# Two of twelve attention chunks rounded later, feature differences moved from GpSimd to VectorE, a feature store and the sums' roundings at other places in the order

## The chip, the cores and the metric

The kernel runs on one core of a Trainium2 chip. The time is device microseconds (us) of one execution, and the time of a kernel is the median of several executions. Engines go by the names of the profile: PE is TensorE, ACT is ScalarE, DVE is VectorE, POOL is GpSimd, SP is the engine that issues nearly all DMAs here. Each engine takes its instructions in the order of the program; an instruction that waits holds up those behind it on its engine.

## The reference

A retention layer (linear attention with a decay per head), then two feed-forward layers on its output. All arithmetic is float32.

```python
for t in range(S):                       # B=2, H=8, S=768, D=64
    state = gamma[None, :, None, None] * state + einsum('bhd,bhe->bhde', k[:, :, t], v[:, :, t])
    y[:, :, t] = scale * einsum('bhd,bhde->bhe', q[:, :, t], state)
x = y.transpose(0, 2, 1, 3).reshape(B * S, H * D)      # 1536 tokens x 512
h = x @ w_in;  x = (h / (1 + exp(-h))) @ w_out         # 512 -> 2048 -> 512
h = x @ moe2_w_in;  return maximum(0.01 * h, h) @ moe2_w_out
```

## The kernel before, in words

The program's order is written out by hand: within an engine, instructions run in the order in which the source issues them, and tiles bring the waits.

**Number format.** A float32 operand is cut into a high part and a rest that PE multiplies separately (`halves`, L199: an ACT copy writes the high part, a DVE subtraction the rest), and three of the four products are taken. The weights arrive as 64-bit words and are turned into float32 on the chip: `words` (L140, two ACT copies, into a buffer of the list `rt` and into the one tile `u`), `clamp` (L148, two DVE operations), `sign` (L159, DVE), `low` (L166, DVE; it reads `u`). `rt` holds three buffers `r`; `rt.pop(0)` takes the one that has been free longest in list order. What is not needed at once goes to a scratch tensor in DRAM (`keep_w`, `keep_s`) and is fetched again (`fetch_w`).

**Stage 1, attention** (to about 52 us): twelve chunks of 128 tokens, two at a time: scores on PE, masking on DVE (L273), values, states and outer products on PE. `store_x` (L355) takes the result of a chunk: for the first six it is scaled by DVE into SBUF (L363), for the last six it stays in PSUM; then it is rounded by `halves`. Chunks 4 and 5 (counting from 0) are the last two of the second set of three, whose halves go to places `w` and `xb`.

**Stage 2, first products of layer 0** (about 52 to 172 us): eight steps, each 256 of the 2048 features for all 1536 tokens. Steps 0 and 1 are computed plainly (`plain`, L863): for each half `p` of the tokens four groups of 12 matmuls, into the two double banks `p0` and `p1` and four single banks `b0` to `b3`. A group's result is read by ACT (L439, the activation); the next step writes the same banks. Steps 2 to 7 (`rest`, L890) use seven products in place of eight: they need sums and differences of weight blocks (`sums`, L192, four operations on POOL) and of the input (`first_t`, `rest_t`, L341 and L346: two operations each, rounded by `split_t`, L351, into `tt`). `up_tasks` (L797) lists what each step does beside its matmuls, by position 0 to 7: a task is issued ahead of the matmuls of its position, and so ahead of the ACT reading of that position's result. Step 1 ends with the first product of step 2 (`n.go(1)`), into the double bank `p0`.

**Stage 3, second products of layer 0** (172 to 304 us) reads the features of a step back from DRAM (`keep` stores them, 1.5 MB; `fetch_g` reads 0.5 MB).

**Stage 4, first products of layer 1** (304 to 426 us): step 0 plain, the others with seven products. In each step `words(w)` of a later weight is at position 2.

**Stage 5, second products of layer 1** (`Two.run`, L561; 426 us to the end): units of about 5.5 us in the first eight, which are plain; the later units use sums of weights that `keep_s` stored, which `ask(k)` fetches into `sf` or `u` and two operations (ACT L648, DVE L654) round.

Of the kernel before, what the change touches and what calls it, by code (L numbers as in the profile page):

```python
# [9 lines left out]
F32 = mybir.dt.float32  # L10
# [8 lines left out]
C = 128  # L19
# [15 lines left out]
PLACES = 6  # L35
NCST = NP * C + C + H + H + NP
# [6 lines left out]
def retention_moe_kernel(ctx: ExitStack, tc: tile.TileContext, att, w1, w2, cst, out):  # L43
# [44 lines left out]
    gate = sb.tile([128, 1], F32, name="gate")  # L88
# [51 lines left out]
    def words(w, which=(0, 1)):  # L140
        t = stage[w]
        if 0 in which:
            r = rs[w] = rt.pop(0)
            nc.scalar.activation(out=r.bitcast(F32), in_=t[:, :, :, 1].bitcast(F32), func=AF.Abs)  # L144
# [47 lines left out]
    def sums(w, which=range(4)):  # L192
        A21, A22, A11, A12 = (blocks(w)[:, n] for n in range(4))
        S1, S2, S3, S4 = (sf[:, n] for n in range(4))
        for o, a, b, op in [((S1, A21, A22, ALU.add), (S3, A11, A21, ALU.subtract),
                             (S2, S1, A11, ALU.subtract), (S4, A12, S2, ALU.subtract))[n] for n in which]:
            nc.gpsimd.tensor_tensor(out=o, in0=a, in1=b, op=op)  # L197
# [157 lines left out]
    def store_x(j):  # L355
# [6 lines left out]
        if j < LATE:  # L362
            nc.vector.tensor_tensor(out=f, in0=y, in1=g4(G), op=ALU.mult)  # L363
            y = f
        if s % 2 == 0:
# [4 lines left out]
        if j >= LATE:  # L370
            nc.scalar.activation(out=f, in_=y, func=AF.Copy)
# [121 lines left out]
    class Two:  # L493
# [67 lines left out]
        def run(self):  # L561
# [67 lines left out]

            for n in range(self.UNITS):  # L630
# [15 lines left out]
                if 1 <= n <= Q:  # L646
                    k = n - 1
# [5 lines left out]
                if 1 <= n <= Q:  # L653
                    nc.vector.tensor_tensor(out=S[k][1], in0=hold[k % 2], in1=S[k][0].bitcast(F32), op=ALU.subtract)  # L654
                for k in range(2) if n == 0 else [n + 1] if n + 1 < Q else []:
                    ask(k)
# [13 lines left out]
    with tc.manual_schedule():  # L670
# [71 lines left out]
        def left_a():  # L742

# [3 lines left out]
            nc.gpsimd.tensor_copy(out=gate, in_=l[:, 1, 511:512].bitcast(F32))  # L747
# [4 lines left out]
            4: lambda: (load_next(), clamp(wb)), 5: lambda: signed(wb),  # L752
# [44 lines left out]
        def up_tasks(layer, k):  # L797
            t = [[] for _ in range(8)]
            at = lambda n, *f: t[n].extend(f)
            if layer == 0 and k < 2:  # L800
                wd = first_w[3]
                if k == 0:
                    at(0, lambda: low(wb), lambda: first_t(0, nc.gpsimd), lambda: rest_t(0, nc.gpsimd))
                    at(1, lambda: words(wc), lambda: split_a(wb))
                    at(2, lambda: clamp(wc), lambda: signed(wc))
                    at(3, lambda: low(wc), lambda: sums(wc))
                    at(4, lambda: split_t(0, 0), lambda: first_t(1, nc.vector))
                    at(6, lambda: split_t(1, 0))
                else:
                    at(0, lambda: split_t(0, 1), lambda: rest_t(1, nc.vector))  # L810
                    at(2, lambda: split_a(wc), lambda: words(wd))
                    at(3, lambda: split_s(wc))
                    at(4, lambda: split_t(1, 1), lambda: clamp(wd))
                    at(5, lambda: signed(wd))
                    at(6, lambda: low(wd), lambda: sums(wd))
                return t
            if layer == 0:
# [5 lines left out]
                if k + 2 < Q:  # L823
# [4 lines left out]
                    at(4, lambda: (low(b), sums(b)), lambda: words(w, (0,)))  # L828
# [14 lines left out]
            if k == 0:  # L843
                at(0, lambda: fetch_w(n), lambda: first_t(1, nc.vector), lambda: rest_t(1, nc.gpsimd))
# [4 lines left out]
                at(7, lambda: split_t(1, 1), lambda: sums(m))  # L849
                return t  # L850
# [242 lines left out]
```

## Time and profile before

| | us |
|---|---|
| median of 3 executions | 559.93 |
| lowest, highest | 558.67, 561.56 |
| the profiled execution, its own time | 561.33 |
| span of the profiled execution, first to last instruction | 559.5 |
| TensorE busy in it | 542.5 |

The own time of the profiled execution lies 1.8 us above its span and 1.4 us above the median. TensorE's granted clock was 0.992 of full speed on average over the span. Busy shares say little of what a change is worth where an engine is nearly always busy; the idle time in front of its instructions, and who ended it, says more.

### The profile page before, as it was taken

The page shows a single profiled execution, that of the slowest core. Times are in us where ns is not written, and L with a number is a line of the kernel's source. Part 1 is how long each engine was busy: PE and PEld are TensorE (multiplying, and loading weights), DVE is VectorE, ACT ScalarE, POOL GpSimd, SP SyncE. Part 2 cuts the span into 40 slices and gives each one's busy share as a digit, 9 for nine tenths or more (in the row PEclk, how much of TensorE's full clock was granted, in tenths as well). Part 3 has the DMA queues.
Part 4 walks back from the last instruction along what each step waited for, and adds up shares of the span by engine and source line. Part 5 has one row for each costly group of instructions (what it writes and reads, how often), then busy time and mean ns, then how long its engine had stood idle before and what let it go on. Part 6 is the DMA issues. An engine that isn't in the chain of part 4 may idle for free.

```text
span 559.5 us, 8890 instructions
## 1 busy us (share of the span) xinstructions
PE 542.5 (97%) x3546; PEld 503.0 (90%) x3546; DVE 417.6 (75%) x546; ACT 301.8 (54%) x367; POOL 104.7 (19%) x92
## 2 busy tenths in 40 slices
PE   7989999999999999999999999998999979999996
PEld 6878999999998788888888999998999858999996
DVE  3798787999956687664867677767877278898993
ACT  2135586777774566644445376646765166443440
POOL 2585322333300000000600662202200000000000
PEclk8999999999999999999999999999999989999999
DMA  8982335778767977889274427776747986642521
GB/s 319 406 336 78 137 127 193 281 266 283 256 227 266 406 237 241 251 289 293 83 255 164 183 114 301 294 293 223 281 150 258 382 311 220 197 136 77 183 82 39
DMA packets 41789, 127.54 MB, mean 228 GB/s; under 512 B 3730, under 2 KB 12050, under 8 KB 39700
## 3 DMA queue, kind: packets, MB, share of 16 engines
q1 hardware_dynamic: 41456, 126.63, 63.8%
q8 instruction: 28, 0.46, 0.3%
q10 hardware_dynamic: 292, 0.34, 0.2%
q14 instruction: 13, 0.11, 0.1%
HBM read 85.01 MB, written 41.94 MB: 227 GB/s over the span
## 4 chain that ended last, share of the span: by engine, by line
PE 58%; DVE 17%; DMA 11%; ACT 5%; issue 5%; POOL 2%; SPq 1%; DVEq 0%; ACTq 0%; POOLq 0%
PE p L394 12%; PE b L394 9%; PE b L602 8%; PE p L471 6%; PE b L471 6%; PE p L602 6%; DMA scr<-r 4%; PE b L878 3%; DVE w L201 3%; DMA c<-g 2%; PE p L878 2%; PE p L586 2%; DVE r L168 2%; PE b L586 2%; DMA sf<-scrs 2%
## 5 line engine op out<-in xcount | busy, mean ns | idle before, releaser
L394 PE MATMUL p<-tt,w 128*128 128x384 f32 x468 | 87.9, 335 | 2.2 <-ACT c L426 2.2
L394 PEld LDWEIGHTS p<-tt,w 128*128 128x128 f32 x468 | 81.8, 188 | 2.9 <-ACT c L426 2.8
L471 PE MATMUL b<-w,wt 128*128 128x512 f32 x216 | 55.1, 390 | 0.5 <-DVE wt L201 0.5
L471 PE MATMUL p<-w,wt 128*128 128x512 f32 x216 | 54.8, 389 | 0.0
L201 DVE TENSOR_TENSOR w<-c,w 128x1024 fp32r<-128x1024 f32 x23 | 29.7, 1293 | 28.9 <-ACT w L200 28.9
L146 ACT ACTIVATE u<-ws 128x1024 int32<-128x1024 uint32 x32 | 36.5, 1139 | 26.3 <-DVE r L168 26.2
L426 ACT ACTIVATE c<-p 128x768 f32<-128x768 f32 x39 | 31.5, 811 | 32.4 <-PE p L394 27.1
L471 PEld LDWEIGHTS b<-w,wt 128*128 128x128 f32 x216 | 40.4, 188 | 9.4 <-DVE wt L201 1.1
L197 POOL TENSOR_TENSOR sf<-r 128x256 f32<-128x256 f32 x26 | 27.7, 1087 | 110.4 <-DVE r L168 59.8
L471 PEld LDWEIGHTS p<-w,wt 128*128 128x128 f32 x216 | 40.5, 188 | 8.4
L161 DVE SCALAR_TENSOR_TENSOR r<-ws,r 128x1024 int32<-128x1024 int32 x32 | 44.3, 1386 | 0.8
L144 ACT ACTIVATE r<-ws 128x1024 f32<-128x1024 f32 x32 | 36.5, 1140 | 13.6 <-DMA scr<-r 7.9
L430 DVE TENSOR_TENSOR big<-b,c 128x384 f32<-128x384 f32 x78 | 39.6, 550 | 5.0 <-ACT c L426 4.6
L168 DVE CUSTOM_DVE_ANT_0 r<-r,u 128x2048 uint16<-128x2048 uint16 x32 | 40.3, 1261 | 0.9
L200 ACT ACTIVATE w<-c 128x1024 fp32r<-128x1024 f32 x23 | 24.4, 1060 | 21.5 <-DMA c<-g 21.5
L201 DVE TENSOR_TENSOR w<-sf,w 128x1024 fp32r<-128x1024 f32 x14 | 17.1, 1225 | 23.3 <-ACT w L200 23.3
L154 DVE TENSOR_SCALAR r<-r 128x1024 int32<-128x1024 int32 x32 | 30.1, 940 | 1.1
L150 DVE TENSOR_SCALAR r<-r 128x1024 f32<-128x1024 f32 x32 | 24.7, 771 | 7.7 <-ACT r L144 7.7
L201 DVE TENSOR_TENSOR w<-r,w 128x768 fp32r<-128x768 f32 (+1 forms) x19 | 22.0, 1159 | 9.9 <-ACT w L200 9.9
L394 PE MATMUL b<-tt,w 128*128 128x384 f32 x156 | 29.2, 335 | 0.0
L394 PE MATMUL p<-xa,w 128*128 128x384 f32 x156 | 29.1, 335 | 0.0
L394 PE MATMUL b<-xb,w 128*128 128x384 f32 x156 | 29.1, 335 | 0.0
(178 smaller groups left out, 1129.7 us busy)
## 6 DMA issues: line engine op xcount, KB each, us to landing
ws<-w_dram SPq DMA_DIRECT2D x64, 512.0 KB, 5.5
g<-big SPq DMA_DIRECT2D x15, 1536.0 KB, 6.9
c<-g SPq DMA_DIRECT2D x30, 512.0 KB, 7.3
att_t<-att_dram SPq DMA_DIRECT2D x20, 512.0 KB, 8.6
scr<-r SPq DMA_DIRECT2D x18, 512.0 KB, 5.9
r<-scr SPq DMA_DIRECT2D x18, 512.0 KB, 5.8
c<-g SPq DMA_DIRECT2D x17, 256.0 KB, 3.4
scrs<-u SPq DMA_DIRECT2D x8, 512.0 KB, 4.0
```

What stands on the lines that cost most here:

```text
L144: nc.scalar.activation(out=r.bitcast(F32), in_=t[:, :, :, 1].bitcast(F32), func=AF.Abs)
L146: nc.scalar.activation(out=u, in_=t[:, :, :, 0].bitcast(U32), func=AF.Copy, scale=2.0 ** -29)
L154: nc.vector.tensor_scalar(out=r, in0=r, scalar1=3, scalar2=0x3FFFFFF8, op0=ALU.logical_shift_left, op1=ALU.bitwise_and,)
L161: nc.vector.scalar_tensor_tensor(out=r, in0=t[:, :, :, 1], scalar=-0x40000000, in1=r, op0=ALU.bitwise_and, op1=ALU.bitwise_or)
L168: nc.vector.tensor_tensor(out=r, in0=r, in1=u, op=ALU.add)
L201: nc.vector.tensor_tensor(out=l, in0=s, in1=h.bitcast(F32), op=ALU.subtract)
L394: nc.tensor.matmul(out=o, lhsT=a[:, ta, k * 128:k * 128 + 128], rhs=rhs(p, tb, k), start=(begin and m == 0), stop=(end and m == 5), skip_g ...
L426: nc.scalar.activation(out=ct[n][:, c, 0:N], in_=t[:, :, 0:N], func=AF.Copy)
L430: nc.vector.tensor_tensor(out=self.block(f, half, c), in0=t[:, :, 0:N], in1=ct[n][:, c, 0:N], op=ALU.add)
L471: nc.tensor.matmul(out=y, lhsT=l, rhs=r, start=(i == 0 and f == 0 and n == 0), stop=(i == Q - 1 and f == 1 and n == 2),)
L602: nc.tensor.matmul(out=y[at][:, 256 * half:256 * half + 256], lhsT=g[:, tg, b], rhs=w[:, tw, a] if sm is None else S[i][tw][:, sm], start= ...
L878: nc.tensor.matmul(out=y[m][0][p][:, 0:N], lhsT=a[:, ta, (A11, A21)[f] + kk // 2, k * 128:k * 128 + 128], rhs=x, start=(i == 0), stop=(i = ...
```

## The change

1. `store_x` of chunks 4 and 5 stops after the scaling into SBUF; a new function `round_x` rounds both after chunk 9, in front of the results of chunks 10 and 11. To make room the clamping of weight `wb` moves behind chunk 11.
2. The differences of the input run on DVE instead of POOL, at other positions (`first_t(0)` and `rest_t(0)` had run on POOL during the end of attention); a one-element POOL copy (`gate`) that held POOL back goes. The weights' sums of steps 2 and 3 run on DVE too (`sums(wc, nc.vector)`, `sums(wd, nc.vector)`); the others stay on POOL. At the start of layer 1 `rest_t(1)` moves from POOL to DVE and the last `split_t` one step back.
3. The features of the last but one step (`steps[6].keep()`) are stored at position 2 of the last step, in both layers, not after it.
4. Two calls of `words` take the buffer that was freed last (`rt.pop(-1)`).
5. In stage 5 the weights' sums are asked for and rounded in units 3 to 7 (`SUMS`, `ASK`), not in units 1 to 8.

```diff
+LATER = (4, 5)
-    def words(w, which=(0, 1)):
+    def words(w, which=(0, 1), at=0):
-            r = rs[w] = rt.pop(0)
+            r = rs[w] = rt.pop(at)
-    def sums(w, which=range(4)):
+    def sums(w, e=None):
-            nc.gpsimd.tensor_tensor(out=o, in0=a, in1=b, op=op)
+            (e or nc.gpsimd).tensor_tensor(out=o, in0=a, in1=b, op=op)
         if j < LATE:
             nc.vector.tensor_tensor(out=f, in0=y, in1=g4(G), op=ALU.mult)
             y = f
+        if j in LATER:
+            return
+        round_x(j, y)
+        if j >= LATE:
+            nc.scalar.activation(out=f, in_=y, func=AF.Copy)
+
+    def round_x(j, y=None):
+        s, c = divmod(j, PER)
+        a, b = c * C, c * C + C
+        if y is None:
+            y = (tm if s % 2 else xf)[s // 2][:, :, :, a:b]
...
+            SUMS = {3: (0,), 4: (1, 2), 5: (3,), 6: (4, 5), 7: (6, 7)}
+            ASK = {1: (0, 1), 3: (2,), 4: (3, 4), 5: (5,), 6: (6, 7)}
-                if 1 <= n <= Q:
-                    k = n - 1
+                for k in SUMS.get(n, ()):
                     nc.scalar.activation(out=S[k][0], in_=hold[k % 2], func=AF.Copy)
...
-                for k in range(2) if n == 0 else [n + 1] if n + 1 < Q else []:
+                for k in ASK.get(n, ()):
                     ask(k)
...
-            4: lambda: (load_next(), clamp(wb)), 5: lambda: signed(wb),
+            4: lambda: (load_next(), [round_x(j) for j in LATER]), 5: lambda: (clamp(wb), signed(wb)),
...
                 if k == 0:
-                    at(0, lambda: low(wb), lambda: first_t(0, nc.gpsimd), lambda: rest_t(0, nc.gpsimd))
+                    at(0, lambda: low(wb))
                     at(1, lambda: words(wc), lambda: split_a(wb))
                     at(2, lambda: clamp(wc), lambda: signed(wc))
-                    at(3, lambda: low(wc), lambda: sums(wc))
-                    at(4, lambda: split_t(0, 0), lambda: first_t(1, nc.vector))
-                    at(6, lambda: split_t(1, 0))
+                    at(3, lambda: low(wc), lambda: sums(wc, nc.vector))
+                    at(4, lambda: first_t(0, nc.vector))
+                    at(5, lambda: split_t(0, 0), lambda: rest_t(0, nc.vector))
+                    at(6, lambda: first_t(1, nc.vector))
+                    at(7, lambda: split_t(0, 1))
                 else:
-                    at(0, lambda: split_t(0, 1), lambda: rest_t(1, nc.vector))
+                    at(0, lambda: split_t(1, 0), lambda: rest_t(1, nc.vector))
+                    at(1, lambda: split_t(1, 1))
                     at(2, lambda: split_a(wc), lambda: words(wd))
                     at(3, lambda: split_s(wc))
-                    at(4, lambda: split_t(1, 1), lambda: clamp(wd))
+                    at(4, lambda: clamp(wd))
                     at(5, lambda: signed(wd))
-                    at(6, lambda: low(wd), lambda: sums(wd))
+                    at(6, lambda: low(wd), lambda: sums(wd, nc.vector))
...
-                    at(4, lambda: (low(b), sums(b)), lambda: words(w, (0,)))
+                    at(4, lambda: (low(b), sums(b)), lambda: words(w, (0,), -1))
...
-                at(0, lambda: fetch_w(n), lambda: first_t(1, nc.vector), lambda: rest_t(1, nc.gpsimd))
+                at(0, lambda: fetch_w(n), lambda: first_t(1, nc.vector), lambda: rest_t(1, nc.vector))
...
-                at(7, lambda: split_t(1, 1), lambda: sums(m))
+                at(7, lambda: sums(m))
                 return t
+            if k == 1:
+                at(0, lambda: split_t(1, 1))
...
-            at(2, lambda: words(w))
+            at(2, lambda: words(w, at=-1))
...
-                    if n:
-                        before.keep()
-                    elif s.layer == 0:
-                        fetch_g(0, 0, 1)
-                    else:
-                        Two.now.fetch(1)
+                    before.keep()
+                    if n is None:
+                        fetch_g(0, 0, 1) if s.layer == 0 else Two.now.fetch(1)
...
-            steps[Q - 2].keep()
```

The matmuls keep their order. Where instructions of other engines now stand is shown at three places. In the rows below a name is a tile with its number, `<-` stands between what is written and what is read, and a line number of the changed kernel is 9 or 10 higher than that of the same line before.

ACT in steps 0 and 1 of stage 2, before: `c` and `big` written from `p` or `b` are the activations of the results in the double and single banks, `tt` the roundings of the differences.

```order
L439 ACTIVATE c<-b_657 128x384
L439 ACTIVATE c<-b_659 128x384
L200 ACTIVATE tt_651<-big_69 128x2x768
L439 ACTIVATE c<-p_655 128x2x384
L439 ACTIVATE c<-p_656 128x2x384
L200 ACTIVATE tt_652<-big_69 128x2x768
L439 ACTIVATE c<-b_658 128x384
L439 ACTIVATE c<-b_660 128x384
```

The same place in the changed kernel (here the double banks are `p_653` and `p_654`, the single ones `b_655` to `b_658`):

```order
L448 ACTIVATE c<-b_655 128x384
L448 ACTIVATE c<-b_657 128x384
L448 ACTIVATE c<-p_653 128x2x384
L200 ACTIVATE tt_649<-big_69 128x2x768
L448 ACTIVATE c<-p_654 128x2x384
L448 ACTIVATE c<-b_656 128x384
L200 ACTIVATE tt_649<-big_68 128x2x768
L448 ACTIVATE c<-b_658 128x384
L200 ACTIVATE tt_650<-big_69 128x2x768
L200 ACTIVATE tt_650<-big_68 128x2x768
L200 ACTIVATE w_651<-r_75 128x768
```

The first rounding of `tt` moved from in front of both double banks' activations to between them, and all four roundings now stand ahead of the activations of step 1.

DVE at the same place in the changed kernel, from the last operation on weight `wc` (L168) on; before, POOL did the first L343 to L349 and the sums (L197), and the first rounding of `tt` followed L168 directly.

```order
L168 ISA r_75<-r_75,u 128x2048
L197 TENSOR_TENSOR sf<-r_75 128x256 x2
L197 TENSOR_TENSOR sf<-sf,r_75 128x256
L197 TENSOR_TENSOR sf<-r_75,sf 128x256
L343 TENSOR_TENSOR big_69<-big_69,big_68 128x768
L344 TENSOR_TENSOR big_69<-big_69 128x768
L201 TENSOR_TENSOR tt_649<-big_69,tt_649 128x2x768
L348 TENSOR_TENSOR big_68<-big_69,big_68 128x768
L349 TENSOR_TENSOR big_68<-big_68,big_69 128x768
L343 TENSOR_TENSOR big_69<-big_69,big_68 128x768
L344 TENSOR_TENSOR big_69<-big_69 128x768
```

The ACT rounding of `tt_649` reads what L344 wrote, so it now stands behind the whole DVE queue up to that L344.

SP from the last step of layer 1 into stage 5, in the changed kernel: `g_6` written from `big` is the store of the last but one step's features, `c<-g` a fetch of features, `r<-scr` one of weights, `sf<-scrs` and `u<-scrs` the first two fetches of sums.

```order
L454 DMA g_6_3462<-big_69 128x3072
L519 DMA c<-g_1_2825 128x2x512
L187 DMA r_75<-scr_1_2_2449 128x1024
L519 DMA c<-g_2_2954 128x2x512
L187 DMA r_2582<-scr_1_3_2760 128x1024
L183 DMA scrs_3524<-u 128x1024
L519 DMA c<-g_3_3083 128x2x512
L454 DMA g_7_3544<-big_68 128x3072
L519 DMA c<-g_4_3212 128x2x512
L187 DMA r_74<-scr_1_4_2889 128x1024
L519 DMA c<-g_5_3340 128x2x512
L187 DMA r_75<-scr_1_5_3018 128x1024
```

Before, `g_6` stood behind `scrs_3524<-u`, in front of `c<-g_3`, and both fetches of sums stood ahead of `c<-g_5`; now they follow `r_75<-scr_1_5`. In layer 0 the store of `g_6` moved in the same way.

## Rows read from the trace of the kernel before

**Rows 1.** The page's busy times, shares of the span and instruction counts.

```profile
PE 542.5 (97%) x3546; PEld 503.0 (90%) x3546; DVE 417.6 (75%) x546; ACT 301.8 (54%) x367; POOL 104.7 (19%) x92
```

**Rows 2.** TensorE's idle time by instruction and releaser: us, times, longest.

```profile
PE b L283 <- DVE c L273: 2.2, 2, 1.8
PE p L394 <- ACT c L426: 2.2, 2, 1.7
PE p L586 <- ACT w L555: 2.1, 1, 2.1
PE p L586 <- DVE w L559: 1.1, 1, 1.1
...
PE b L471 <- DVE wt L201: 0.5, 1, 0.5
```

**Rows 3.** Busy us by window: PE, PEld, DVE, ACT, POOL, clock, DMA.

```profile
440.00:460.00 20.00, 16.74 (x66) 13.14 (x65) 9.37 (x9) 8.87 (x10) 0.00 (x0) 0.91 0.91 337
452.00:454.00 2.00, 2.00 (x5) 1.61 (x6) 2.00 (x2) 2.00 (x3) 0.00 (x0) 0.50 0.92 280
```

**Rows 4.** Timeline of DVE in attention: start, us, instruction, idle before.

```profile
33.91 0.94 DVE L201 TENSOR_TENSOR w<-big,w 128x256 fp32r<-128x256 f32 x1 [0.48 <-ACT w L200]
...
35.52 1.10 DVE L150 TENSOR_SCALAR r<-r 128x1024 f32<-128x1024 f32 x1
...
38.81 2.34 DVE L273 TENSOR_TENSOR c<-p,c 128x1024 f32<-128x1024 f32 x2
```

**Rows 5.** Timeline of DVE at the start of stage 2.

```profile
57.11 0.42 DVE L201 TENSOR_TENSOR xb<-b,xb 128x256 fp32r<-128x256 f32 x1 [0.45 <-ACT xb L200]
...
62.15 1.23 DVE L201 TENSOR_TENSOR w<-r,w 128x1024 fp32r<-128x1024 f32 x1 [2.20 <-ACT w L200]
63.29 0.69 DVE L150 TENSOR_SCALAR r<-r 128x1024 f32<-128x1024 f32 x1
...
66.00 1.23 DVE L168 CUSTOM_DVE_ANT_0 r<-r,u 128x2048 uint16<-128x2048 uint16 x1
...
75.47 1.76 DVE L201 TENSOR_TENSOR tt<-big,tt 128x1536 fp32r<-128x1536 f32 x1 [0.38 <-ACT tt L200]
77.15 0.95 DVE L348 TENSOR_TENSOR big<-big,big 128x768 f32<-128x768 f32 x1
78.02 0.95 DVE L349 TENSOR_TENSOR big<-big,big 128x768 f32<-128x768 f32 x1
```

**Rows 6.** Timeline of ACT in the same stage.

```profile
64.14 1.50 ACT L439 ACTIVATE c<-p 128x768 f32<-128x768 f32 x2
71.82 1.49 ACT L200 ACTIVATE tt<-big 128x1536 fp32r<-128x1536 f32 x1 [6.17 <-DVE big L344]
73.21 0.85 ACT L439 ACTIVATE c<-b 128x384 f32<-128x384 f32 x2
...
75.34 0.83 ACT L200 ACTIVATE w<-r 128x768 fp32r<-128x768 f32 x1
...
79.46 0.50 ACT L439 ACTIVATE big<-b 128x384 f32<-128x384 f32 x1
```

**Rows 7.** Timeline of PE there: step 1's first groups, step 2's first product.

```profile
68.74 4.32 PE L878 MATMUL p<-xa,w 128*128 128x384 f32 x24
...
83.32 2.24 PE L394 MATMUL p<-xa,w 128*128 128x384 f32 x12
```

**Rows 8.** Groups of instructions by shape: busy us, mean ns; VectorE and GpSimd.

```profile
L181 DVE TENSOR_TENSOR u<-r 128x256 f32<-128x256 f32 x16 | 6.1, 422 | 0.3
...
L343 POOL TENSOR_TENSOR big<-big,big 128x768 f32<-128x768 f32 x2 | 3.7, 1831 | 120.3 <-DVE b L201 120.3
```

**Rows 9.** Timeline of ACT in stages 4 and 5: long waits for DMAs.

```profile
376.46 1.12 ACT L144 ACTIVATE r<-ws 128x1024 f32<-128x1024 f32 x1 [3.76 <-DMA scr<-r]
...
447.24 1.06 ACT L648 ACTIVATE s<-sf 128x1024 fp32r<-128x1024 f32 x1 [8.14 <-DMA sf<-scrs]
```

**Rows 10.** The page's DMA issues: KB each, median us from issue to landing.

```profile
g<-big SPq DMA_DIRECT2D x15, 1536.0 KB, 6.9
```

More of the change, by code (lines that the diff above doesn't have):

```diff
@@ L87, in retention_moe_kernel @@
     z1 = sb.tile([128, 1], F32, name="z1")
-    gate = sb.tile([128, 1], F32, name="gate")
     one = sb.tile([1, 64], F32, name="one")
@@ L195, in sums @@
         for o, a, b, op in [((S1, A21, A22, ALU.add), (S3, A11, A21, ALU.subtract),
-                             (S2, S1, A11, ALU.subtract), (S4, A12, S2, ALU.subtract))[n] for n in which]:
-            nc.gpsimd.tensor_tensor(out=o, in0=a, in1=b, op=op)
+                             (S2, S1, A11, ALU.subtract), (S4, A12, S2, ALU.subtract))[n] for n in range(4)]:
+            (e or nc.gpsimd).tensor_tensor(out=o, in0=a, in1=b, op=op)
     def halves(h, l, s):
@@ L369, in store_x @@
             halves(*put(s, a, b, 1)[0:2], y[:, 1])
-        if j >= LATE:
-            nc.scalar.activation(out=f, in_=y, func=AF.Copy)
     TERMS = ((0, 0), (0, 1), (1, 0))
@@ L652, in run @@
                     self.left(n + 2)
-                if 1 <= n <= Q:
+                for k in SUMS.get(n, ()):
                     nc.vector.tensor_tensor(out=S[k][1], in0=hold[k % 2], in1=S[k][0].bitcast(F32), op=ALU.subtract)
-                for k in range(2) if n == 0 else [n + 1] if n + 1 < Q else []:
+                for k in ASK.get(n, ()):
                     ask(k)
@@ L746, in left_a @@
             rt.append(rs.pop(wa))
-            nc.gpsimd.tensor_copy(out=gate, in_=l[:, 1, 511:512].bitcast(F32))
         amid = {2: lambda: words(wa), 4: low_a}
```

## The prediction

> **What bounds the kernel now.** I read the page's busy times first. TensorE works 542.5 us of a span of 559.5 [rows 1], so 17 us of idle time is all that an unchanged order of matmuls can still lose, apart from the clock. The list of TensorE's waits by releaser says where some of it lies: 1.8 in attention behind a masking on VectorE, 1.7 behind an ACT copy, 0.5 behind a rounding of `wt`, and 2.1 and 1.1 at one place in stage 5 [rows 2]. The clock adds to the last of these: after it a window of 2 us was granted 0.50 of full speed (1.2 of 2.4 GHz), and the 20 us around it 0.91 [rows 3]. The timelines of the other engines then tell what each of these waits waited for, and how much room VectorE has where work is added. The sum below is made against the profiled execution's own 561.33; its result is 1.4 lower on the scale of the median. Times are those of the execution before; where an early saving shifts TensorE and VectorE alike, I leave it out of both.
>
> **Attention, −1.8.** The second roundings of chunks 4 and 5 go from the place where the clamping of `wa` waits for them: VectorE has them from 33.91 on, 0.94 for one, and the clamping starts at 35.52 [rows 4]. Two of these just ahead of it are 1.6 to 1.9 us; the masking at 38.81 in the same queue [rows 4] comes so much sooner, which is all of the wait of 1.8 behind it [rows 2]. The roundings come back behind chunk 9, four of 0.42 on VectorE each behind an ACT copy. There the clamping of `wb` makes room. Spread over the ping-pong of ACT and VectorE they end some 2.5 to 3.5 us after 51.1, before TensorE asks for these features behind its first 24 matmuls of stage 2. So they cost nothing here; if they were late, TensorE would lose what they are late. The last rounding of chunk 11 ended at 57.5 before [rows 5], and I take 57.0, between 56.3 and 58.0, as its end now.
>
> **The start of stage 2, +7.1.** This is the term that decides. VectorE now has in one row what GpSimd did beside it. I follow its queue:
>
> - 57.0: clamping, sign and low part of `wb`. The same four operations on `wc` go from 63.29 to 67.23 [rows 5], 3.94 us: 60.9.
> - ACT must write `u` and the high part before the subtraction can start. That wait is 2.20 before [rows 5]: 63.1. The subtraction takes 1.14 to the start of the next instruction: 64.2.
> - The same four for `wc`, 3.94: 68.2.
> - The weights' sums, four operations on 128x256. VectorE has no such sum here, but the row of L181 has its shape: 0.42 each [rows 8], some 1.5 to 1.7 in a row: 69.7.
> - `first_t(0)`, L343 and L344 on 128x768. VectorE took 0.95 for L348, and 0.87 from its start to that of L349 [rows 5]: 1.8 for two, 71.5.
> - ACT may then round `tt`, 1.49 [rows 6]: 73.0. Behind it in ACT's queue stands, since the change, the reading of the second double bank. Two such readings take 1.50 [rows 6], so one about 0.75: 73.8.
>
> TensorE wants to write that bank with the second 12 of the 24 matmuls that begin at 68.74 and take 4.32 [rows 7]; half of it is 2.1, so at 70.8. **First stall: 3.0.** Before, both readings stood ahead of that `tt`, at 64.14 [rows 6].
>
> What is late next is the rest of the chain, since all four `tt` now stand ahead of the readings of step 1. VectorE: subtraction for `tt`, 1.76 [rows 5], to 74.8; `rest_t(0)`, 1.8, to 76.6; `first_t(1)`, 1.8, to 78.4; two subtractions, 1.7 each, to 81.9; `rest_t(1)`, 1.8, to 83.7. ACT's fourth `tt` is then done at 85.2. Behind it stand six instructions (rounding of `w`, two of `words`, two readings of single banks, rounding of a sum), from 75.34 to the end of the one at 79.46 before [rows 6]: 4.5 to 4.6, so 89.7. Then comes the reading of the first double bank, 0.75: 90.4. TensorE wants this bank for step 2's first product, at 83.32 before [rows 7]; with the first stall 86.3. **Second stall: 4.1.** Together TensorE is 7.1 late. Every other bank and weight of that step is ready by then. Errors of 1 us in the start of the chain go through both stalls once.
>
> Is that queue as strict as I take it? The row of ACT at 71.82 says so: the rounding of `tt` waited 6.17 us for L344, and the readings of single banks that follow it begin only at 73.21 [rows 6]. The Trainium skill, "PSUM — Partial Sum Buffer", section "Engine vs sequencer instructions", has it as a rule that the queues of ScalarE, VectorE and GpSimd are strictly first in, first out; the trace agrees, and by the rule alone the new order costs whatever L344 is late.
>
> **The clock behind it, +1.7.** The only row with a wait of this size in mid-kernel is the one in stage 5: 3.2 us of waits, and then a share of 0.91 over 20 us [rows 2, 3], 1.8 lost. I take 1.7 for the stall of 4.1, and keep 0 (the clock stays) to 3.4 (both stalls bring it down).
>
> **Stores sooner, −0.5.** The next-to-last step's store goes six positions earlier, so the first transfers of the stage behind can land sooner. In stage 3 the wait for `wt` is 0.5 [rows 2]. I take it as gone; bounds 0 and −0.7.
>
> **The buffer of `words`, −1.7.** An ACT copy of weights waited 3.76 us for the store out of its buffer [rows 9]; behind it on ACT is the copy L426, for which TensorE waited 1.7 [rows 2]. The buffer freed last has no such store pending. Bounds 0 (this wait may be of the profiled execution alone) and −1.7.
>
> **Layer 1's start, −0.5.** The other 0.5 of that line [rows 2] is where GpSimd's late sums hold ACT up; with `rest_t(1)` on VectorE, GpSimd has 3.7 less of its slow operations (1.83 each [rows 8]). Bounds 0 and −0.5.
>
> **Sums of stage 5, −4.9.** ACT waited 8.14 us at 447.24 for the first fetch of sums [rows 9], and TensorE for ACT and VectorE behind it 2.1 and 1.1 [rows 2]; the clock lost 1.8 over those 20 us [rows 3], of which I take 1.7, since the rest of the span is not quite at full speed either. The rounding now comes two units, 11 us, later, and the fetch moves behind only a few other transfers. Bounds −3.2 and −4.9.
>
> **Sum.** −1.8 +7.1 +1.7 −0.5 −1.7 −0.5 −4.9 = −0.6: 560.7 as the profiled execution's own time, **559.3** on the scale of the median. The parts nearly cancel: 9.4 gained at five places and 8.8 lost at one.
>
> **Rivals.**
> *VectorE keeps up.* Neither stall nor its clock: 559.93 − 9.4 = 550.5. It needs L344 to end at 68.5, 3.0 sooner than I have it. For it speaks that several operations before were slow while GpSimd worked beside them: GpSimd took 1.83 for what VectorE does in 0.95 [rows 5, 8], and that is gone now. Against: the 3.94 for four operations are of a stretch without any such slowness, and the 2.20 of the wait for ACT stays. The Trainium skill, "GPSIMD Engine Reference", section 4.1 "Engine selection", advises VectorE for elementwise work with two inputs, as GpSimd is about half as fast; the trace agrees with the ratio, and by that advice alone the move is a gain. It says nothing of a queue that is already full.
> *Only the first stall.* If the last `tt` comes sooner than I have it (ACT's six instructions partly ahead, or operations of 0.9 rather than 0.95 all along), the second stall shrinks away, and with it the clock's part: 559.93 − 9.4 + 3.0 = 553.5. The chain would have to be 4 us shorter between 71.5 and 90.4.
> *Slower: a store ahead of the first fetch.* The 1.5 MB of the next-to-last step's features took 6.9 us to land [rows 10]; in layer 1 this store now stands ahead of the fetch of the second unit's features on SP's queue, and in layer 0 likewise. If that fetch lands later by this store's 6.9 and had only some 4 us to spare, each of the two stages starts with a wait of 2 to 3 us: 559.3 + 4.5 = 563.8. It decides from the point where the store is issued less than a unit (5.5 us) ahead of the fetch. Against it: the store starts while TensorE is still in the last step's middle.
>
> **How the numbers follow.** The forecast has 0.50, VectorE keeping up 0.12, only the first stall 0.16, the slower case 0.22. The predicted time is the forecast's, 559.3; its own range, with the bounds of the clock, of the buffer and of the chain's start, is 556.5 to 562.5. Eight times in ten asks for the first-stall case and the slower one too: 553 to 564. About 0.5% (2.8 us) is what a measurement can tell from no change: from 557.1 to 562.7. Faster: 0.12, 0.14 of the first-stall case and 0.06 of the forecast's tail, 0.32. Slower: 0.16 of the slower case and 0.05 of the forecast's tail, 0.21. The rest, 0.47, is the same.
>
> **What would show it.** Right: in TensorE's list of waits the 1.8 behind the masking, the 1.7 of the copy and the 2.1 and 1.1 of stage 5 are gone, and two new ones stand at the start of stage 2 (some 66 to 88), of about 3 and 4 us, both released by ACT's reading of a double bank, with a clock near 0.5 for a few us after the second. Wrong: no such wait there (then VectorE's L344 ends below 68.5, or ACT's queue is not what I read), a wait for features at the first units of stages 3 or 5, or ACT still waiting for fetched sums in stage 5.

## The result: 1.1% slower

The changed kernel takes 565.94 us (median of 8 executions, 563.93 to 568.53), the kernel before in the same session 559.64 (8 executions). The ratio is 1.0111, with a 95% interval of 1.0073 to 1.0149. The forecast was 559.3 with a range of 553 to 564, most likely no change.

The profiled execution of the changed kernel took 568.07, 2.1 above the kernel's median and 6.7 more than that of before. First its busy times and its clock in 40 slices:

```profile
PE 547.3 (97%) x3546; PEld 507.8 (90%) x3546; DVE 419.8 (74%) x560; ACT 302.4 (53%) x367; POOL 82.9 (15%) x77
...
PEclk9999998999999999999999999999999999799999
```

TensorE is busy 4.8 us longer with the same 3546 matmuls [rows 1], so some of them ran at a lower clock: the two slices below 9 are at 85 to 99 us and at 481 to 495. The list of TensorE's waits by releaser (us, times, longest) says what stands ahead of them:

```profile
PE p L611 <- ACT w L564: 3.4, 1, 3.4
PE p L891 <- ACT c L448: 3.2, 1, 3.2
PE p L403 <- ACT big L448: 2.1, 1, 2.1
...
PE b L480 <- DVE wt L201: 0.6, 1, 0.6
PE p L611 <- DVE w L568: 0.5, 1, 0.5
PE b L283 <- DVE c L273: 0.4, 1, 0.4
```

Of the waits of before [rows 2], the 1.8 behind the masking, the 1.7 behind the copy and the 2.1 and 1.1 in stage 5 are gone, as forecast. The two behind ACT's readings of the double banks (L448) are the forecast ones. The first line is not: it belongs to L611, the seven products of the second half of stage 5.

Since the matmuls keep their order, the start of the same matmul can be compared in the two timelines. The difference says by how much the changed kernel's stands behind (+) or ahead (−), in us:

| the same matmul | before | after | difference | gained or lost since the line above |
|---|---|---|---|---|
| attention, ahead of all that is changed | 14.32 | 12.69 | −1.6 | −1.6 |
| first of stage 2 | 51.55 | 47.01 | −4.5 | −2.9 |
| step 1, first double bank | 68.74 | 63.86 | −4.9 | −0.3 |
| step 2, second product | 87.48 | 91.78 | +4.3 | +9.2 |
| stage 3, behind the wait for `wt` | 190.38 | 195.95 | +5.6 | +1.3 |
| layer 1, in its first steps | 323.99 | 329.15 | +5.2 | −0.4 |
| layer 1, behind the wait for the copy | 380.11 | 383.65 | +3.5 | −1.6 |
| stage 5, ahead of the sums | 432.22 | 436.08 | +3.9 | +0.3 |
| stage 5, behind the old waits | 454.98 | 453.88 | −1.1 | −5.0 |
| stage 5, unit 10 under way | 482.73 | 488.74 | +6.0 | +7.1 |
| the last matmul | 554.03 | 560.67 | +6.6 | +0.6 |

The first line is not the change's: three of the four kernels below that leave attention as it was have it as well (1.45 to 1.55). In the profiled execution of before TensorE stood at half speed for a stretch early in attention, as this window of it shows (its granted clock is the third number from the end):

```profile
11.20:14.50 3.30, 3.30 (x50) 3.18 (x47) 1.16 (x1) 0.04 (x1) 1.73 (x2) 0.50 1.02 413
```

The fourth of these kernels, stores_only, has such a stretch at the same place. What was won or lost since the line above is free of it, from the second line on.

**The start of stage 2.** TensorE's timeline of the changed kernel (start, us, instruction, idle before), which answers to [rows 7]:

```profile
63.86 2.25 PE L891 MATMUL p<-xa,w 128*128 128x384 f32 x12
69.35 3.92 PE L891 MATMUL p<-xa,w 128*128 128x384 f32 x12 [3.25 <-ACT c L448]
...
85.92 3.78 PE L403 MATMUL p<-xa,w 128*128 128x384 f32 x12 [2.15 <-ACT big L448]
```

Twelve such matmuls take 2.25; behind each wait they take 3.92 and 3.78. What ACT and VectorE did, which answers to [rows 5, 6]:

```profile
67.12 1.48 ACT L200 ACTIVATE tt<-big 128x1536 fp32r<-128x1536 f32 x1 [7.19 <-issue]
68.51 0.79 ACT L448 ACTIVATE c<-p 128x768 f32<-128x768 f32 x1
...
79.16 1.49 ACT L200 ACTIVATE tt<-big 128x1536 fp32r<-128x1536 f32 x1 [3.56 <-DVE big L349]
80.56 0.83 ACT L200 ACTIVATE w<-r 128x768 fp32r<-128x768 f32 x1
...
85.08 1.49 ACT L448 ACTIVATE big<-p 128x768 f32<-128x768 f32 x2
```

```profile
52.03 0.42 DVE L201 TENSOR_TENSOR xb<-b,xb 128x256 fp32r<-128x256 f32 x1 [0.45 <-ACT xb L200]
...
66.08 0.96 DVE L344 TENSOR_TENSOR big<-big 128x768 f32<-128x768 f32 x1
...
78.18 0.95 DVE L349 TENSOR_TENSOR big<-big,big 128x768 f32<-128x768 f32 x1
```

ACT's queue stood 7.2 us before its first `tt` (the trace names no releaser there, but VectorE ended the input, L344, at 67.04, and ACT began at 67.12), and behind it stood the reading `c<-p` for which TensorE waited. From the last rounding of chunk 11 (52.45) to L344's end are 14.6 us; the prediction had 14.5. The second time the queue stood 3.56 us for `rest_t(1)`, then had 4.5 us of other work ahead of `big<-p`, as worked out.

**Stage 5.** ACT's timeline of the changed kernel there: L658 rounds a fetched sum, L671 copies results out, L564 rounds the features of unit 10 and later ones.

```profile
453.46 1.05 ACT L658 ACTIVATE s<-sf 128x1024 fp32r<-128x1024 f32 x1
...
467.62 1.06 ACT L658 ACTIVATE w<-sf 128x1024 fp32r<-128x1024 f32 x1 [1.24 <-DMA sf<-scrs]
470.64 1.07 ACT L658 ACTIVATE w<-u 128x1024 fp32r<-128x1024 f32 x1 [1.96 <-DMA u<-scrs]
...
474.86 1.06 ACT L658 ACTIVATE w<-sf 128x1024 fp32r<-128x1024 f32 x1 [2.31 <-DMA sf<-scrs]
478.86 1.06 ACT L658 ACTIVATE s<-u 128x1024 fp32r<-128x1024 f32 x1 [2.94 <-DMA u<-scrs]
479.82 1.06 ACT L671 ACTIVATE o<-p 128x512 f32<-128x512 f32 x2
...
481.73 0.97 ACT L564 ACTIVATE w<-r 128x896 fp32r<-128x896 f32 x1
```

The first sum no longer waits (8.14 before [rows 9]). But from the fourth sum on the waits grow (0.85, 1.24, 1.96, 2.31, 2.94), and the last, in unit 7, holds up ACT until 478.86. Behind it in the queue are the copies and the rounding of unit 10's features. TensorE ran through units 8 and 9 meanwhile, whose features were rounded, and stood still at 479.3:

```profile
482.75 0.58 PE L611 MATMUL p<-wt,w 128*128 128x256 f32 x1 [3.44 <-ACT w L564]
483.88 1.44 PE L611 MATMUL p<-wt,w 128*128 128x256 f32 x5 [0.55 <-DVE w L568]
```

SP's timeline says why the last sum was late. Its fetch goes into the buffer `u`, which the sum two before it had held until VectorE was done reading it at 472.97:

```profile
472.99 0.33 SPq L585 DMA_DIRECT2D u<-scrs  x1
```

Issued at 472.99, used at 478.86: 5.9 us, where a unit lasts 5.5. The windows behind the three waits (TensorE's granted clock is the third number from the end):

```profile
69.30:73.10 3.80, 3.75 (x12) 3.75 (x13) 3.77 (x5) 1.32 (x2) 0.00 (x0) 0.55 0.02 4
...
85.90:89.40 3.50, 3.48 (x12) 3.48 (x13) 3.40 (x5) 1.04 (x2) 0.00 (x0) 0.58 0.00 0
...
482.70:488.00 5.30, 4.70 (x20) 4.41 (x21) 5.13 (x10) 1.78 (x2) 0.00 (x0) 0.50 0.88 268
```

In each of them TensorE was at half speed, 1.2 of 2.4 GHz, most of the time: the granted clock is 0.50 all through from 69.40 to 72.80, from 86.50 to 89.80 and from 482.40 to 489.20.

### The profile page after: what moved, and what is told of

It is laid out like the page before. It is cut to its first block, busy times and chain, and to the rows that moved or that the text cites. A ratio compares the mean times of both kernels' runs of the same rounds, so it can differ in the third digit from the quotient of the medians.

```text
span 566.2 us, 8866 instructions
## 1 busy us (share of the span) xinstructions
PE 547.3 (97%) x3546; PEld 507.8 (90%) x3546; DVE 419.8 (74%) x560; ACT 302.4 (53%) x367; POOL 82.9 (15%) x77
## 4 chain that ended last, share of the span: by engine, by line
PE 65%; DVE 12%; DMA 9%; ACT 6%; issue 5%; SPq 1%; DVEq 0%; ACTq 0%
PE p L403 18%; PE b L403 13%; PE b L611 7%; PE p L480 7%; PE b L480 7%; PE p L611 6%; DMA c<-g 2%; DMA r<-scr 2%; DVE w L201 2%; DMA u<-scrs 2%; PE b L283 2%; PE b L891 2%; DVE r L168 1%; DMA att_t<-att_dram 1%; PE p L266 1%
## 5 line engine op out<-in xcount | busy, mean ns | idle before, releaser
L197 POOL TENSOR_TENSOR sf<-r 128x256 f32<-128x256 f32 x22 | 21.9, 1016 | 175.8 <-DVE r L168 78.9
L161 DVE SCALAR_TENSOR_TENSOR r<-ws,r 128x1024 int32<-128x1024 int32 x32 | 42.7, 1334 | 0.8
L168 DVE CUSTOM_DVE_ANT_0 r<-r,u 128x2048 uint16<-128x2048 uint16 x32 | 40.4, 1261 | 0.9
L403 PE MATMUL p<-xa,w 128*128 128x384 f32 x156 | 30.9, 349 | 2.4 <-ACT big L448 2.1
L403 PEld LDWEIGHTS p<-xa,w 128*128 128x128 f32 x156 | 28.5, 195 | 3.0 <-ACT big L448 2.5
L403 PE MATMUL b<-xa,w 128*128 128x384 f32 x156 | 29.3, 337 | 0.0
L154 DVE TENSOR_SCALAR r<-r 128x1024 int32<-128x1024 int32 x32 | 27.4, 856 | 1.1
```

Source lines behind the costliest of these rows:

```text
L154: nc.vector.tensor_scalar(out=r, in0=r, scalar1=3, scalar2=0x3FFFFFF8, op0=ALU.logical_shift_left, op1=ALU.bitwise_and,)
L161: nc.vector.scalar_tensor_tensor(out=r, in0=t[:, :, :, 1], scalar=-0x40000000, in1=r, op0=ALU.bitwise_and, op1=ALU.bitwise_or)
L168: nc.vector.tensor_tensor(out=r, in0=r, in1=u, op=ALU.add)
L403: nc.tensor.matmul(out=o, lhsT=a[:, ta, k * 128:k * 128 + 128], rhs=rhs(p, tb, k), start=(begin and m == 0), stop=(end and m == 5), skip_g ...
```

## The experiments

The kernels of each group below ran on one chip with the kernel before, whose median was 560.0 to 560.2 in all three groups. Ratios are to it, with 95% intervals; two kernels, of different groups or not, are compared by their ratios, so differences in per cent are of before's time (1% is 5.6 us). The changed kernel stands at 1.0111.

### First group: the two places of loss, and attention alone

**last8.** In the changed kernel:

```diff
-            SUMS = {3: (0,), 4: (1, 2), 5: (3,), 6: (4, 5), 7: (6, 7)}
+            SUMS = {3: (0,), 4: (1, 2), 5: (3,), 6: (4, 5), 7: (6,), 8: (7,)}
```

> The changed kernel with one entry moved: the last of the eight sums of weights is rounded in unit 8 of stage 5, behind ACT's copies of the first results and the rounding of unit 10, not in unit 7. Theory (the new stall of 3.4 + 0.5 us at the start of the second half of stage 5, and the half clock behind it, come from the fetch of this last sum, behind which ACT's queue stands): the stall and its clock go, 7 us less than the changed kernel, so about 559. Rival (TensorE waits there for the features of unit 10 themselves, or the wait is of the profiled execution alone): within 2 us of the changed kernel, 564 to 568.

562.43 us, 1.0035 (1.0009 to 1.0060): 0.76% less than the changed kernel, 4.3 us. ACT's timeline of this kernel, at the same place:

```profile
475.03 1.06 ACT L658 ACTIVATE w<-sf 128x1024 fp32r<-128x1024 f32 x1 [1.91 <-DMA sf<-scrs]
476.00 1.06 ACT L671 ACTIVATE o<-p 128x512 f32<-128x512 f32 x2
...
477.90 0.97 ACT L564 ACTIVATE w<-r 128x896 fp32r<-128x896 f32 x1
479.09 1.06 ACT L658 ACTIVATE s<-u 128x1024 fp32r<-128x1024 f32 x1 [0.21 <-DMA u<-scrs]
```

The features of unit 10 are rounded 3.8 us sooner, and TensorE's wait of 3.44 is gone; 0.5 and 0.6 behind VectorE are left. From 454.98 to 482.73 on the clock of before this kernel loses 1.9 us where the changed one lost 7.1, 5.2 less in the traces. The theory holds; 7 was too much, since some waiting stays.

**old2.** The changed kernel with the tasks of steps 0 and 1 of stage 2, and the gate, as before:

```diff
-                    at(0, lambda: low(wb))
+                    at(0, lambda: low(wb), lambda: first_t(0, nc.gpsimd), lambda: rest_t(0, nc.gpsimd))
...
-                    at(5, lambda: split_t(0, 0), lambda: rest_t(0, nc.vector))
-                    at(6, lambda: first_t(1, nc.vector))
-                    at(7, lambda: split_t(0, 1))
+                    at(4, lambda: split_t(0, 0), lambda: first_t(1, nc.vector))
+                    at(6, lambda: split_t(1, 0))
...
```

> The changed kernel with steps 0 and 1 of stage 2 as before (differences of the input and sums of step 2 on GpSimd, at the old positions, with the gate). Theory: the two stalls behind ACT's readings of the double banks (3.2 and 2.1 us) and the half clock behind each (1.8 and 1.6 us) go, 9 us less than the changed kernel, so about 557. Rival (GpSimd beside the later roundings of chunks 4 and 5 slows VectorE, or the stalls are given back at step 2): 3 us less or none, 563 to 566.

561.09 us, 1.0006 (0.9983 to 1.0029): 5.9 us less than the changed kernel, between theory and rival. The waits of 3.2 and 2.1 became 0.5 and 2.2. So the old order makes TensorE wait in front of step 2 too, once it arrives sooner than before.

**old2_last8.** Both edits.

> Both edits at once. Theory: the two places are independent, so the gains add, 16 us less than the changed kernel and some 10 less than before: 549 to 551. Rival (part of the gain is given back at the next wait, or the throttle takes it back in clock): 553 to 558.

556.34 us, 0.9932 (0.9908 to 0.9955): faster than before. The gain of the one edit stands beside that of the other (0.74% from old2 to this). The sum of 16 us fails, because each was too large.

**attn.** The kernel before with the first part of the change alone:

```diff
+LATER = (4, 5)
...
+        if j in LATER:
+            return
+        round_x(j, y)
...
-            4: lambda: (load_next(), clamp(wb)), 5: lambda: signed(wb),
+            4: lambda: (load_next(), [round_x(j) for j in LATER]), 5: lambda: (clamp(wb), signed(wb)),
```

> The kernel before with only the roundings of chunks 4 and 5 moved behind chunk 9 and the clamping of wb behind chunk 11. Theory: the wait of 1.8 us behind the masking goes and with it some of what lies around it, 2 to 3 us less than before: 557. Rival (with GpSimd still at work on the differences beside them, the moved roundings are late for stage 2): equal to before or slower, 559 to 562.

561.75 us, 1.0022 (0.9998 to 1.0046): nothing gained, the rival's time. But the theory's mechanism is in the trace: TensorE starts stage 2 at 47.68, 3.9 us sooner than in the trace of before (1.4 of it from the half clock early in that one). Then it gives this back, in its timeline of this kernel:

```profile
65.23 4.42 PE L888 MATMUL p<-xa,w 128*128 128x384 f32 x24 [0.52 <-ACT c L449]
73.66 4.32 PE L888 MATMUL p<-xa,w 128*128 128x384 f32 x24
82.28 2.35 PE L404 MATMUL p<-xa,w 128*128 128x384 f32 x12 [2.21 <-ACT big L449]
```

Step 2 starts at 82.28, 1.0 sooner than before [rows 7], which is less than that 1.4. What is late for stage 2 is not the roundings, as the rival had it, but ACT's readings. One part of why is that VectorE is slower there while GpSimd works on the differences: its clamping and sign of `wb` take 2.23 and 2.75. In the changed kernel they take 0.69 and 1.23; the low part behind them ends at 56.31 there and at 60.16 in attn, 3.9 us later, of which these two are 3.1. The same place in old2_last8, which has the same attention and the same old tasks, with GpSimd's operations beside VectorE's:

```profile
54.05 2.22 DVE L155 TENSOR_SCALAR r<-r 128x1024 int32<-128x1024 int32 x1
56.31 2.75 DVE L162 SCALAR_TENSOR_TENSOR r<-ws,r 128x1024 int32<-128x1024 int32 x1
...
53.54 2.18 POOL L349 TENSOR_TENSOR big<-big,big 128x768 f32<-128x768 f32 x1
55.68 2.31 POOL L350 TENSOR_TENSOR big<-big,big 128x768 f32<-128x768 f32 x1
```

Without GpSimd beside them VectorE's two take 0.69 and 1.23 (in the same kernel at 64.39 and 65.12).

### Second group: is it the order in the queue, or VectorE's load?

**tt_both.** In the changed kernel the roundings `tt` stand behind ACT's readings of the double banks; the subtraction on VectorE that belongs to each moves with it, and nothing else does:

```diff
-                    at(5, lambda: split_t(0, 0), lambda: rest_t(0, nc.vector))
-                    at(6, lambda: first_t(1, nc.vector))
+                    at(5, lambda: rest_t(0, nc.vector))
+                    at(6, lambda: split_t(0, 0), lambda: first_t(1, nc.vector))
...
-                    at(1, lambda: split_t(1, 1))
...
-                    at(6, lambda: low(wd), lambda: sums(wd, nc.vector))
+                    at(6, lambda: split_t(1, 1), lambda: low(wd), lambda: sums(wd, nc.vector))
```

> The changed kernel with two roundings of differences moved behind ACT's readings of the double banks: the first from position 5 to 6 of step 0, the last from position 1 to 6 of step 1. The work of every engine stays the same. Theory (the two stalls come from where the roundings stand in ACT's queue, in front of readings that would long be possible, and not from VectorE being full): the waits of 3.2 and 2.1 us behind ACT's readings shrink to under 1 us each and the half clock behind them goes, 6 to 9 us less than the changed kernel, 557 to 560. Rival (VectorE's chain is simply too long, and TensorE then waits for the rounded differences themselves or for the weights behind them): 2 us less or none, 564 to 567, with new waits at step 2's first products.

559.72 us, 0.9977 (0.9956 to 0.9998): 1.34% or 7.5 us less than the changed kernel. TensorE's timeline of this kernel, and ACT's:

```profile
64.20 4.33 PE L890 MATMUL p<-xa,w 128*128 128x384 f32 x24
72.58 4.33 PE L890 MATMUL p<-xa,w 128*128 128x384 f32 x24
79.66 2.35 PE L403 MATMUL p<-xa,w 128*128 128x384 f32 x12 [0.64 <-ACT big L448]
```

```profile
59.46 1.54 ACT L448 ACTIVATE c<-p 128x768 f32<-128x768 f32 x2
...
78.78 1.52 ACT L448 ACTIVATE big<-p 128x768 f32<-128x768 f32 x2
80.16 1.52 ACT L200 ACTIVATE tt<-big 128x1536 fp32r<-128x1536 f32 x1
```

Both readings of the first pair are done at 61.0, where the changed kernel had the second at 69.3. One wait of 0.64 is left, and the granted clock from 60 to 100 us is 1.00. Step 2 starts 3.7 us ahead of before; 1.6 of this is before's half clock in attention, so some 2 of the 2.9 won in attention are kept. VectorE does the same work, so its load was not the limit: ACT's queue stood behind an instruction that had to wait. The wait at unit 10 is still in this trace, 3.5.

**stage2.** The kernel before with the second part of the change alone, in steps 0 and 1 (all tasks there as in the change, and no gate):

```diff
-                    at(0, lambda: low(wb), lambda: first_t(0, nc.gpsimd), lambda: rest_t(0, nc.gpsimd))
+                    at(0, lambda: low(wb))
...
+                    at(5, lambda: split_t(0, 0), lambda: rest_t(0, nc.vector))
+                    at(6, lambda: first_t(1, nc.vector))
+                    at(7, lambda: split_t(0, 1))
...
```

> The kernel before with only the second part of the change, in steps 0 and 1 of stage 2 (differences and the sums of steps 2 and 3 on VectorE, at the new positions, without the gate). Theory (stalls as in the changed kernel, but TensorE reaches them some 2 to 3 us later, since attention is not shortened): 4 to 7 us more than before, 564 to 567. Rival (the stalls need the moved roundings of chunks 4 and 5): within 1.5 us of before.

568.32 us, 1.0138 (1.0106 to 1.0170): slower by 7.7, a little above the theory's range. The rival falls. Of the two stalls the first is only 0.7 here, since TensorE comes later to it; the second, behind the reading of `big<-p`, is 3.7, with 12 matmuls at 0.50 of the clock behind it.

**old2_last8_tt.** In old2_last8, the same idea for the old order:

```diff
-                    at(4, lambda: split_t(0, 0), lambda: first_t(1, nc.vector))
+                    at(5, lambda: split_t(0, 0), lambda: first_t(1, nc.vector))
...
-                    at(4, lambda: split_t(1, 1), lambda: clamp(wd))
+                    at(4, lambda: clamp(wd))
...
-                    at(6, lambda: low(wd), lambda: sums(wd))
+                    at(6, lambda: split_t(1, 1), lambda: low(wd), lambda: sums(wd))
```

> The changed kernel with steps 0 and 1 of stage 2 as before, the last sum of stage 5 in unit 8, and two roundings of differences behind ACT's readings of the double banks (positions 4 to 5 in step 0 and 4 to 6 in step 1). Theory: the waits of 0.6 and 2.2 us behind these readings, which are left in the run without this last edit, go: 2 to 3 us less than that run's 556.3, so 553.5 to 554.5. Rival (the next thing in the chain is as late, the rounded differences or step 2's weights): 556.

555.98 us, 0.9917 (0.9887 to 0.9946): the rival's time, and no difference from old2_last8 that can be measured. The wait of 0.6 is gone, that of 2.2 is 1.7. ACT's queue still stands 6.2 us for a difference, until 73.12; two `tt` (to 76.7) and six other instructions are then ahead of the reading, which comes at 81.13, only 0.45 sooner than in old2_last8.

**sums_only.** The kernel before with the fifth part alone:

```diff
+            SUMS = {3: (0,), 4: (1, 2), 5: (3,), 6: (4, 5), 7: (6, 7)}
+            ASK = {1: (0, 1), 3: (2,), 4: (3, 4), 5: (5,), 6: (6, 7)}
```

> The kernel before with only the fifth part of the change: in stage 5 the weights' sums are asked for and rounded in units 3 to 7. Theory (5 us gained at units 2 to 3, and 5 to 7 us lost at unit 10 behind the fetch of the last sum): equal to before or up to 2 us slower, 560 to 562. Rival (the late fetch needs the sooner stores or the other order of transfers of the whole change): 5 us faster, 555.

562.05 us, 1.0030 (1.0006 to 1.0054): a little slower, as the theory had it. TensorE waits 3.5 and 0.5 at unit 10, as in the changed kernel. So the stall at unit 10 needs no other part of the change.

### Third group: the mends together, and the stores

**tt_both_last8.** The edits of tt_both and last8 together.

> The changed kernel with both mends: two roundings of differences behind ACT's readings of the double banks (as in the run before, 559.7) and the last sum of stage 5 in unit 8. Theory (two independent places): the stall of 3.5 and 0.5 us at unit 10 and its clock go, 4 to 5 us less than 559.7, so 554.5 to 556, the fastest so far or equal to it. Rival (the throttle or the transfers give it back): 557 to 559.

554.56 us, 0.9908 (0.9885 to 0.9931): the fastest, 1.0% faster than before and 2.0% faster than the changed kernel. TensorE's longest wait past attention is 0.9, and its busy time is 541.6.

**tt_both_last8_nostore.** The same, with the store after the last step again:

```diff
-                    before.keep()
+                    if n:
+                        before.keep()
...
+            steps[Q - 2].keep()
```

> The same with the features of the last but one step stored as before, after the last step, in both layers. Theory (stored sooner they delay the first fetches of stage 3, where the traces show 1 us lost instead of 0.5): 0.5 to 1 us less than the run with the sooner stores. Rival (the sooner store brings its 0.5 us, as predicted): 0.5 us more.

554.72 us, 0.9909 (0.9888 to 0.9930): no difference. By the time neither the theory nor the rival is shown; an effect of 0.5 is too small for this. The traces say more about the place: from step 2's second product to the matmul behind the wait for `wt` (87.48 to 190.38 in before's) the eight kernels that store sooner take 104.0 to 105.8 us, the six that do not 102.9 to 103.6. There the sooner store loses about 1 us, and this kernel against the one above shows 1.3.

**stores_only.** The kernel before with the third part alone, that is with the lines of the last diff the other way round.

> The kernel before with only the third part of the change, the features of the last but one step stored sooner in both layers. Theory (a small loss at the start of stage 3): 0 to 1 us more than before. Rival of the prediction (0.5 us gained behind the wait for wt): 0.5 less. Rival of its slower case (each stage's first units wait 2 to 3 us for their features): 4 to 5 more.

558.20 us, 0.9975 (0.9951 to 0.9998): 1.4 us faster, with an interval that nearly reaches no change. On the whole time the theory of a loss falls (the loss of 1 us is in the trace at its place, but not in the median), and the slower case of the prediction with it. Where the gain comes from I leave open: the wait of 0.5 for `wt` is still there, 0.6, and in stage 5 the wait of 2.1 [rows 2] is 1.2 in this trace with the clock at 1.00 behind it, but the pair above shows no gain in a kernel that has no such wait.

**sums8_only.** The kernel before with the fifth part, and the last sum in unit 8 as in last8.

> The kernel before with the fifth part of the change, but the last sum in unit 8. Theory: the waits of 2.1 and 1.1 us and the half clock behind them go and none takes their place: 4 to 5 us less than before, 555.5. Rival (the transfers are as late at another unit): 558 to 560.

557.72 us, 0.9977 (0.9948 to 1.0005). Against sums_only it is 0.53% or 3.0 us less; the two intervals just miss each other. By the start of the same matmul its trace gains 2.7 on that of before from layer 1 (378.02 against 380.11) to the end (549.27 against 554.03). The old waits are gone, but 0.7, 0.5 and 0.4 are left at the later units, and the median moved by 2.3 where the theory had 4 to 5.

## Why the prediction was wrong

**Attention, −1.8: right in the mechanism, sized too small.** 2.9 us in the profiled pair. It is a gain only as long as stage 2 can take it. Alone (attn) it is given back; with the readings in front of the roundings (tt_both) some 2 us of it are kept. In the sum it could stand as a gain of its own, because the stall behind it was worked out with VectorE's chain shifted by as much.

**The start of stage 2, +7.1, and the clock, +1.7: right.** 9.2 measured against 8.8. The first stall was 3.25 (3.0 forecast), the second 2.15 (4.1), since the half clock came behind both and made TensorE late for the second by itself; it cost 1.7 each time. The upper bound of the clock's term, 3.4, was the true one, and the second stall shrank by about as much as the clock took in front of it. That ACT's queue decides was shown by tt_both. The rule that the Trainium skill gives in "PSUM — Partial Sum Buffer", section "Engine vs sequencer instructions", that ScalarE's queue is first in, first out, is borne out by that pair: the same instructions with two of them behind the readings cost 7.5 us less. The rival in which VectorE keeps up was wrong on the time of L344, which came to within 0.1 us of the chain's length.

**Stores, −0.5: not shown.** The wait for `wt` stayed at 0.6 (0.5 before [rows 2]), and the stretch that ends with it is longer in every trace with the sooner store than in any without, by about 1 us, not shorter. In the time, alone the part may be worth 1.4, in the mended kernel nothing.

**The buffer of `words`, −1.7: right in the mechanism, sized by one execution.** ACT waits for the store out of its buffer in the traces of all six kernels with the old buffers, from 1.52 us in stores_only to 3.76 in before, and in none of the eight with the buffer freed last. But how much of it reaches TensorE differs: at the matmul where before waits 1.65, stage2 waits 1.03, sums_only 0.43, sums8_only 0.33, attn and stores_only not at all. In stage2's trace the two waits are:

```profile
382.66 1.12 ACT L143 ACTIVATE r<-ws 128x1024 f32<-128x1024 f32 x1 [3.18 <-DMA scr<-r]
386.31 2.35 PE L393 MATMUL p<-tt,w 128*128 128x384 f32 x12 [1.03 <-ACT c L425]
```

So the 1.7 was the largest of six values, and half of the six are under 0.4. The lower bound, 0, was kept for this reason. No run has the buffers changed alone.

**Layer 1's start, −0.5:** 0.4 in the pair, and no run tells it apart.

**Sums of stage 5, −4.9: the step that failed.** The old waits went, and −5.0 is what the pair shows there. Part of it is the clock of one execution: in the traces of stage2 and stores_only, which keep the old order there, the clock stays at 1.00 and the same stretch is 1.5 and 2.0 us shorter than in before's, so that the term's smaller bound, −3.2, fits them. That is a matter of size.

The step that failed is another. The prediction said "the fetch moves behind only a few other transfers" and looked at the first fetch alone. Eight sums through two buffers, in five units in place of eight, have a last fetch too. It is issued when its buffer is free, takes 5.9 us, and ACT's queue stands behind it with the rounding of unit 10's features. That wait, 3.4 and 0.5, with the half clock behind it, costs 7.1 in the pair. No term and no rival had it; only the last sign of being wrong, "ACT still waiting for fetched sums in stage 5", named it. Moving this one rounding by one unit gives back 0.76, 0.74, 0.69 and 0.53% in four pairs of kernels (3.0 to 4.3 us), so over many executions it seems to cost less than in the profiled one, although some of the loss stays in the mended kernels (1.9 in last8's trace).

With 3 to 7 us for it the sum would have been 2.4 to 6.5 slower, and 6.3 was measured. last8, the change without most of this loss, is still 2.0 slower than before where the sum had 0.6 faster; the buffer's and the stores' terms, which fell short, and the rest of the loss are of that size, but no run divides it among them.

The range ended at 564 because its slower end was built on another mechanism, the store ahead of a fetch, which stores_only does not bear out.

## What to carry to other kernels

When a chain of fetches through few buffers is moved or made denser, follow its last fetch with the same care as its first: from the moment its buffer comes free, through its landing, to what stands behind it in the waiting engine's queue. In an in-order queue, put an instruction that will wait behind all those that could already run and that someone waits for; here the same work cost 9 us in one trace and a wait of 0.6 in the other, 7.5 by the medians. A stage that is shortened only pays if the next stage does not wait for another engine whose chain has not moved.

## What was not expected of the hardware

The clock did not fall after every wait of some 2 us. Behind waits of 3.25 and 3.44 the granted clock was 0.55 and 0.50, and 0.58 behind one of 2.15 that began 14 us after the end of the first. But in attn, behind a wait of 2.21 at the same place with only one of 0.52 ahead of it in the stage, it was 1.00:

```profile
82.30:84.60 2.30, 2.30 (x13) 2.30 (x14) 2.27 (x3) 1.01 (x2) 0.00 (x0) 1.00 0.00 0
```

Stage 5 of the old order has the same: behind 2.1 and 1.1 in before and behind 1.8 and 1.1 in attn the clock fell to 0.50, behind 1.7 and 1.1 in stage2 and behind 1.2 and 1.1 in stores_only it stayed at 1.00. Two executions with nearly the same waits can thus differ by more than a microsecond, and a term that takes its clock from a single one is uncertain by as much.

And VectorE's operations on `r` took 2.22 and 2.75 us beside GpSimd's differences, 0.69 and 1.23 without. The Trainium skill, "SBUF — State Buffer", section "Who interferes with whom", tells that VectorE and GpSimd share a pair of ports and that, when both need it, one waits for the other; these rows agree, since each slow operation of VectorE ends only after the operation of GpSimd beside it (56.27 against 55.72, 59.06 against 57.99). The prediction took the fast times for the changed kernel, 3.94 for the four operations on `wb`, and the trace bears this out, but it named the gain only in a rival.
